# Gate and value of a second pair of blocks as a 2x2 block product with seven products

## The chip, the cores and the metric

The kernel runs on one core of a Trainium2 chip. Its time is the device time of one execution in microseconds (us); the kernel before takes 939.78 us, the median of 3 runs (939.59 to 940.44).

## The reference

Three steps in a row over 4 batches of 576 tokens (2304 rows of 512). *Attention*, 8 heads of 64: a pooled part (queries, keys and values averaged over 4 tokens, full softmax, result repeated 4 times) plus a local part (each token sees 3 tokens to each side). *First layer pair*: `h = x @ w_in` (512 to 2048), `g = max(h,0) + alpha*min(h,0)`, `x = g @ w_out`. *Second layer pair*: rows divided by their root mean square and multiplied by `rms_g`, then `gate = xn @ w_gate`, `val = xn @ w_val` (512 to 1536), result `(gate * sigmoid(gate) * val) @ w_out`. All inputs and the output are float32.

## The kernel before, in words

**Blocks.** The 2304 tokens are 6 blocks of 384; activations lie with features on the 128 partitions and tokens along the free dimension. Each float32 factor is held as two float16 halves, high and low, so a product of one 128-row slice is three matmuls (high x high, high x low, low x high).

**Layer one** (`m1`) takes a block through 16 groups of 128 hidden features: 12 matmuls of 384 columns into a bank `hps` (L1462), the activation, a split into halves `ghl` (L441, L442) and 12 matmuls into four accumulators `acc` (L1479). **Layer two** (`m2`) takes a block through 12 groups f: 12 gate and 12 value matmuls of 384 columns (`gps`, L1602), the gate (L1615 and L1616 with tanh, L1587 with silu), the value (L1619), a split `uhl` (L1622, L1623) and 9 output matmuls of 512 columns into `oacc` (L1631). Its input is first normalised (`rms_tasks`; L1434 to L1437: product, high half, low half).

**Blocks 4 and 5** go through layer two together in `m2_pair`. Gate and value weights over two halves of the 512 features form a 2x2 matrix of blocks, and the halves of the two token blocks another. Their product takes seven block products of 6 matmuls instead of eight for each f (L1825, banks `pa`, `pb`, `pf`), from four sums of weight blocks (`pair_w`, a call for each of four weight tiles; GpSimd makes the full weights L1740, VectorE the differences L1745, ScalarE and VectorE the halves L1668, L1669) and four sums of input blocks (`pair_x`, L1687). After the products come copies out of PSUM on ScalarE (L1830), additions on VectorE (L1833), two silu gates (L1587) and two values (L1841). The output matrix is a seven-product form too (L1803, L1804, L1810, L1813, L1850 to L1858 make its sums; L1908 its products).

**Attention** fills the other engines meanwhile. Blocks 2 to 5 need chunks `local(4)` to `local(11)` of 192 tokens, two for each block: GpSimd multiplies queries with keys (L547) and weights with values (L601), VectorE reduces (L558, L614), TensorE transposes, VectorE adds the pooled part (L650), and ScalarE and VectorE write the block's input `xt` in halves (L441, L442). `down(b)` is the pooled attention of batch b. Chunks, pooled heads and weight loads take turns in three buffers `raw`; `xt` has two.

**Order.** The program order is: layer one of blocks 0 and 1, layer two of 0 and 1, layer one of 2 and 3, layer two of 2, layer one of 4 and 5, layer two of 3, `m2_pair`. The dictionary `feed` gives attention and weight work to a stage, `rms_at` the normalisation. Afterwards `issue_order` puts every engine's instructions in a fixed order: a list scheduler with its own table of costs, whose priorities are path lengths to the end, corrected by the table `LEADS` (range of instruction numbers, ns).

Of the kernel before, what the change touches and what calls it, by code (L numbers as in the profile page):

```python
# [2114 lines left out]
```

## Time and profile before

| | us |
|---|---|
| median of 3 runs | 939.78 |
| the profiled execution | 936.82 |
| its span, first to last instruction | 935.1 |
| TensorE busy | 909.3 |
| VectorE busy | 662.0 |
| ScalarE busy | 520.4 |
| GpSimd busy | 337.7 |

Busy times are sums over the records of an engine. PE is TensorE, PEld its weight loads, DVE VectorE, ACT ScalarE, POOL GpSimd, SP SyncE. A matmul's record includes its way through the array, so records overlap; how far apart they start tells what each costs in a stream. The stages of the second half, from the timeline: layer one of blocks 2 and 3 from 393 us, layer two of 2 from 533, layer one of 4 and 5 from 600 and 665, layer two of 3 from 732, the pair's gates and values from 802, its outputs until the end.

### The profile page before, as it was taken

To read this page: it belongs to the slowest core of one execution; us is meant where nothing else is said; L and a number is where in the kernel's file an instruction comes from. 1 tells how busy PE (TensorE), PEld (TensorE's weight loads), DVE (VectorE), ACT (ScalarE), POOL (GpSimd) and SP (SyncE) were. 2 spreads that over 40 slices of the span, in tenths; PEclk is the share of its full clock that TensorE was granted. 3 is DMA by queue.
4 is the path that set the end of the run, shared out by engine and by line. 5 is a ranking of instruction groups with operands and counts; after the bars stand their busy time and mean duration, and the time that the engine had idled before them with its cause. 6 is when DMAs were issued, how large, how long until landed. Compare 5 with 4: busy or idle time off the path is not lost.

```text
span 935.1 us, 16829 instructions
## 1 busy us (share of the span) xinstructions
PE 909.3 (97%) x6574; PEld 608.4 (65%) x6574; DVE 662.0 (71%) x1257; ACT 520.4 (56%) x1222; POOL 337.7 (36%) x279
## 2 busy tenths in 40 slices
PE   7979999999999999999999999999999999999997
PEld 5768777799755555566666655556666555566686
DVE  4789996797989965788765777387366234478882
ACT  5899999889973365133576232243444332465640
POOL 1101100350436304777224788252132010057750
PEclk9999999999999999999999999999999999999999
DMA  9785445455321232221131211010000000000002
GB/s 243 242 281 171 128 114 178 157 192 195 102 85 60 69 108 70 85 85 60 60 119 36 85 51 34 2 33 1 1 1 1 1 1 1 23 12 1 1 1 68
DMA packets 53713, 73.80 MB, mean 79 GB/s; under 512 B 22190, under 2 KB 35138, under 8 KB 53634
## 3 DMA queue, kind: packets, MB, share of 16 engines
q1 hardware_dynamic: 53634, 72.74, 25.2%
q8 instruction: 51, 0.84, 0.4%
q14 instruction: 28, 0.23, 0.1%
HBM read 68.01 MB, written 4.72 MB: 78 GB/s over the span
## 4 chain that ended last, share of the span: by engine, by line
PE 86%; DMA 4%; ACT 4%; DVE 3%; issue 1%; SPq 0%; POOL 0%; DVEq 0%; ACTq 0%
PE gps L1602 20%; PE acc L1479 18%; PE hps L1462 18%; PE oacc L1631 9%; PE pa L1825 4%; PE px L1908 3%; DMA out_dram<-ob 2%; PE pf L1825 2%; PE py L1908 1%; PE pb L1825 1%; DMA wr<-in_moe_w_in_dram 1%; PE sps L734 1%; PE avps L774 1%; PE lsps L957 1%; DMA wr<-in_moe_w_gate_dram 1%
## 5 line engine op out<-in xcount | busy, mean ns | idle before, releaser
L1462 PE MATMUL hps<-xt,wi 128*128 128x192 f16 (+1 forms) x1536 | 342.0, 289 | 4.1 <-DVE ghl L442 1.2
L1479 PE MATMUL acc<-ghl,wo 128*128 128x384 f16 (+1 forms) x960 | 245.1, 310 | 0.9 <-DVE x L1565 0.4
L1602 PE MATMUL gps<-x,w 128*128 128x384 f16 x1152 | 238.1, 326 | 0.0
L1462 PEld LDWEIGHTS <-wi 128*128 128x128 f16 x1536 | 148.4, 100 | 59.7 <-issue 6.7
L1479 PEld LDWEIGHTS <-wo 128*128 128x128 f16 x1344 | 128.8, 98 | 57.6 <-issue 0.8
L1602 PEld LDWEIGHTS <-w 128*128 128x128 f16 x1152 | 112.5, 99 | 75.5 <-issue 1.4
L1631 PE MATMUL oacc<-w,uhl 128*128 128x512 f16 x432 | 139.7, 379 | 0.0
L547 POOL TENSOR_TENSOR prod<-cq,ckv 128x896 f32<-128x896 f32 x48 | 100.4, 2111 | 74.7 <-PE avps L774 50.8
L1468 DVE SCALAR_TENSOR_TENSOR hps<-g,oma,hps 128x192 f32<-128x192 f32 (+1 forms) x128 | 66.2, 518 | 46.2 <-ACT g L1466 45.5
L601 POOL TENSOR_TENSOR prod<-ls,ckv 128x896 f32<-128x896 f32 x48 | 84.7, 1853 | 28.7 <-DVE lo L614 26.2
L1466 ACT ACTIVATE g<-hps 128x384 f32<-128x384 f32 x96 | 47.2, 491 | 77.4 <-PE hps L1462 76.8
L1631 PEld LDWEIGHTS <-uhl 128*128 128x128 f16 x432 | 42.6, 99 | 41.2 <-ACT uhl L1622 0.2
L1479 PE MATMUL acc<-g,wo 128*128 128x384 f16 (+1 forms) x384 | 68.8, 286 | 0.0
L441 ACT ACTIVATE ghl<-hps,grp 128x384 f16<-128x384 f32 (+1 forms) x73 | 42.1, 577 | 31.9 <-DVE hps L1468 31.4
L442 DVE SCALAR_TENSOR_TENSOR ghl<-hps,grp,ghl 128x384 f16<-128x384 f32 (+1 forms) x73 | 44.3, 607 | 19.0 <-ACT ghl L441 18.9
L558 DVE TENSOR_REDUCE ls<-prod 128x14 f32<-128x896 f32 x48 | 51.7, 1079 | 3.4 <-POOL prod L547 3.3
L614 DVE TENSOR_REDUCE lo<-prod 128x128 f32<-128x896 f32 x48 | 51.8, 1080 | 2.3 <-POOL prod L601 2.0
L1615 ACT ACTIVATE th<-gps,tsc 128x384 f32<-128x384 f32 x36 | 20.7, 579 | 58.7 <-PE gps L1602 58.7
L987 POOL TENSOR_TENSOR dls<-dls,dlsum 96x408 f32<-96x408 f32 x12 | 11.8, 1005 | 110.2 <-ACT g L441 61.4
L1740 POOL TENSOR_TENSOR wt<-w 128x768 f32<-128x768 f16 x16 | 27.4, 1712 | 66.3 <-ACT g L1466 30.4
L1622 ACT ACTIVATE uhl<-gps 128x384 f16<-128x384 f32 x48 | 23.4, 487 | 44.5 <-DVE gps L1619 39.4
L1187 ACT ACTIVATE wr<-wr 128x768 f32<-128x768 f32 (+1 forms) x48 | 42.0, 879 | 4.2 <-DMA wr<-in_moe_w_in_dram 2.1
(332 smaller groups left out, 1682.6 us busy)
## 6 DMA issues: line engine op xcount, KB each, us to landing
wr<-in_moe_w_out_dram SPq DMA_DIRECT2D x18, 512.0 KB
wr<-in_moe_w_in_dram SPq DMA_DIRECT2D x10, 768.0 KB
wr<-in_moe_w_gate_dram SPq DMA_DIRECT2D x8, 768.0 KB
wr<-in_moe_w_val_dram SPq DMA_DIRECT2D x8, 768.0 KB
ckv<-in_k_dram SPq DMA_DIRECT2D x7, 768.0 KB
ckv<-in_v_dram SPq DMA_DIRECT2D x7, 768.0 KB
wr<-in_moe_w_out_dram SPq DMA_DIRECT2D x20, 256.0 KB
sd<-in_q_dram SPq DMA_DIRECT2D x24, 144.0 KB
```

The costliest lines, as they stand in the source:

```text
L442: nc.vector.scalar_tensor_tensor(out=lo, in0=src, scalar=s, in1=hi, op0=ALU.mult, op1=ALU.subtract)
L547: engs[i].tensor_tensor(out=pr, in0=view(st["q"][:, j, t:t + TP], [[D, TP], [0, ND], [1, D]]), in1=view(st["k"][:, j, t:t + TP], [[D, TP], ...
L558: nc.vector.tensor_reduce(out=st["s"][:, j, t:t + TP], in_=st.pop(("p", i)), axis=AX.X, op=ALU.add)
L601: engs[i].tensor_tensor(out=over(pr, i), in0=view(st["s"][:, j, t:t + TP], [[ND, TP], [1, ND], [0, D]]), in1=view(st["v"][:, j, t:t + TP], ...
L614: nc.vector.tensor_reduce(out=st["o"][:, t:t + TP, j], in_=view(pr, [[ND * D, TP], [ND, D], [1, ND]]), axis=AX.X, op=ALU.add)
L1462: nc.tensor.matmul(ps[:, j], wi[:, f + j, a, kk * 128:(kk + 1) * 128], x[:, b_, kk, c0:c0 + n], start=(i == 0), stop=(i == 3 * KK - 1))
L1466: nc.scalar.activation(out=g, in_=ps, func=AF.Relu, scale=-1.0)
L1468: nc.vector.scalar_tensor_tensor(out=ps[:, j], in0=g[:, j], scalar=oma[:, f + j:f + j + 1], in1=ps[:, j], op0=ALU.mult, op1=ALU.add)
L1479: nc.tensor.matmul(acc[e], wo_f(f)[:, a, e * 128:(e + 1) * 128], hl[:, b_], start=(f == f0 and i == 0), stop=(f == f1 and i == 2))
L1602: nc.tensor.matmul(ps, w2_t[i0 + f // 3].rearrange("p a (k c) -> p a k c", k=KK)[:, a, kk, (f % 3) * 128:(f % 3 + 1) * 128], xh[:, b_, kk] ...
L1631: nc.tensor.matmul(acc[tt], t[:, a, tt * 128:(tt + 1) * 128], w[:, b_, f % 3], start=(f in first and i == 0), stop=(f in last and i == 2))
L1825: nc.tensor.matmul(ps, w[:, a, kk, c:c + 128], x[:, b_, kk], start=(start and n == 0), stop=(n == 3 * K2 - 1), skip_group_check=True)
```

## The change

Blocks 2 and 3 become a pair as well (`m2_pair_a`). Their gate and value products take the seven-product form through `pair_f`, which is the loop body of the old `m2_pair` made a function; their outputs are plain products, made after all twelve f from halves kept in `wo`. `m2` is left for blocks 0 and 1. Layer one of blocks 2, 3, 4 and 5 follows in one row, then `m2_pair_a`, then `m2_pair`. The sums of the weight blocks are made once and used by both pairs: the first weight tile's in layer one of block 5, the other three in the first groups of `m2_pair_a`, with scratch in `wo`. `pair_x(p)` makes the normalised inputs and their differences for a pair in pieces of 384 columns; `rms_tasks` of blocks 2 to 5 leaves a copy of the norm factor in SBUF (`r_t`) and no longer multiplies. Block 2's gate is silu in place of tanh. `local(10)` is handed over one stage earlier. Scratch of `m2_pair` moves to other buffers, and `LEADS` is another table (328 entries for 262).

```diff
@@ -22,59 +22,72 @@
 LEADS = (
-    (8269, 8277, -4000), (3290, 3494, -500), (6599, 6626, -500), (7948, 7994, -15500), (5847, 6045, -12500),
...
@@ -1369,6 +1382,8 @@
 
     x1_t = {}
 
+    PAIR = 2
+
             st["r"] = ps
+            if m >= PAIR:
+                st["r"] = r_t[m] = att.tile([128, BW], F32, tag=("xs", "aT")[m % 2], name="rs")
+                nc.scalar.activation(out=r_t[m], in_=ps, func=AF.Copy)
...
-        return [sq(e) for e in range(KK)] + [ssum, bcast] + [xn(e) for e in range(KK)]
+        return [sq(e) for e in range(KK)] + [ssum, bcast] + [xn(e) for e in range(KK) if m < PAIR]
-            tag = ("x1", "xh", "u11")[m % 3]
+            tag = ("x1", "xh", "u11", "x1", "xh", "raw")[m]
-            if m == PAIR - 1:
-                silu(u, gp, f)
-            else:
-                nc.scalar.activation(out=th, in_=gp, func=AF.Tanh, scale=tsc[:, f // 3:f // 3 + 1])
-                nc.vector.scalar_tensor_tensor(out=u, in0=th, scalar=1.0, in1=gp, op0=ALU.add, op1=ALU.mult)
+            nc.scalar.activation(out=th, in_=gp, func=AF.Tanh, scale=tsc[:, f // 3:f // 3 + 1])
+            nc.vector.scalar_tensor_tensor(out=u, in0=th, scalar=1.0, in1=gp, op0=ALU.add, op1=ALU.mult)
...
+    def pair_x(p):
+        ma, mb = PAIR + 2 * p, PAIR + 2 * p + 1
+        last = mb == NBLK - 1
+        st = {}
+
+        def begin():
+            for m in (ma, mb):
+                xh_t[m] = x1_t[m].bitcast(F16).rearrange("p k (a n) -> p a k n", a=2)
+            if p == 0:
+                t12 = xt_p.tile([128, 2, 2, K2, BW], F16, tag="xt", name="xc")
+                t4 = att.tile([128, 2, K2, BW], F16, tag="lo", name="xc")
+                tx[p] = {1: t12[:, 0], 2: t12[:, 1], 3: xh_t[mb][:, :, 0:K2], 4: t4}
+            else:
+                tx[p] = {n: w2_t[3 + n][:, :, 0:PW].rearrange("p a (k n) -> p a k n", k=K2) for n in range(1, 5)}
+
...
+        def y(k, n):
+            def f():
+                if k == n == 0:
+                    begin()
+                if n == 0:
+                    st["y"] = place(k)
+                m, e = (ma, mb)[n // 2], k + K2 * (n % 2)
+                o = st["y"][n]
+                for i in range(NT if m == mb and last else 1):
+                    z = [o, x1_t[m][:, e], r_t[m]]
+                    if m == mb and last:
+                        z = [v[:, i * 128:(i + 1) * 128] for v in z]
+                        z = [z[0].rearrange("p (c t) -> p t c", c=NC)] + [
+                            v.rearrange("p (t c) -> p t c", c=NC) for v in z[1:]]
+                    nc.vector.scalar_tensor_tensor(out=z[0], in0=z[1], scalar=rgx[:, e:e + 1], in1=z[2],
+                                                   op0=ALU.mult, op1=ALU.mult)
+                if n != 2:
+                    halves(xh_t[m][:, 0, e], xh_t[m][:, 1, e], o)
+            return f
+
+        def diff(k, n):
+            def f():
+                b11, b21, b12, b22 = st["y"]
+                o, a, b = ((b11, b12, b11), (b11, b22, b11), (b12, b22, b12), (b21, b21, b11))[n - 1]
+                nc.vector.tensor_tensor(out=o, in0=a, in1=b, op=ALU.subtract)
+                halves(tx[p][n][:, 0, k], tx[p][n][:, 1, k], o)
+            return f
+
+        NT = BW // 128
+        return [t for k in range(K2) for t in [y(k, n) for n in range(4)] + [diff(k, n) for n in range(1, 5)]]
...
+            if i:
+                o = (6 + n) * 2 * BW
+                return wo[:, o:o + PW]
...
+    def pair_f(p, f, scr, done):
...
+        product(A, wv(i, 0), b11, c, True)
+        snap(s1_, A)
+        product(B_, wv(i, K2), b21, c, True)
+        plus(s1_, B_)
+        ga = gate(f, s1_, wk, "mm")
+        product(A, s[1], t[2], c, False)
+        snap(s2_, A)
+        product(F_, s[0], t[1], c, True)
+        product(A, s[2], t[3], c, False)
+        snap(s3_, A)
+        plus(s3_, F_)
+        product(F_, s[3], b22, c, False)
+        plus(s2_, F_)
+        gb = gate(f, s2_, hl_p, "hl")
+        product(A, wv(4 + i, K2), t[4], c, False)
+        done(f, ga, A, gb, s3_)
...
+    def m2_pair_a():
         ma, mb = PAIR, PAIR + 1
         NT = BW // 128
-        scr = [outd_p.tile([128, BW], F32, tag="outd", name="sn") for _ in range(2)]
+        free, scr = ring()
+        ut = xt_p.tile([128, 2, 2, BW], F32, tag="xt", name="uhl")
+        free.extend([outd_p.tile([128, BW], F32, tag="outd", name="sn") for _ in range(2)])
+        spare = [ut[:, 1, 0], ut[:, 1, 1]]
+        free.extend(spare + val_places(0))
+
+        def uhl(f):
+            t = wo[:, f * 2 * BW:(f + 1) * 2 * BW] if f < 10 else ut[:, f - 10].rearrange("p h n -> p (h n)")
+            return t.bitcast(F16).rearrange("p (h a n) -> p h a n", h=2, a=2)
+
+        def done(f, ga, A, gb, s3_):
+            for h, (u, v) in enumerate(((ga, A), (gb, s3_))):
+                value(f, u, u, v)
+                t = uhl(f)[:, h]
+                halves(t[:, 0], t[:, 1], u)
+
+        w_tasks = deque(t for i in (1, 2, 3) for t in pair_w(i))
+        r_tasks = deque(rms_tasks(ma + 2) + rms_tasks(mb + 2))
+        for f in range(NF2):
+            for _ in range(8):
+                if w_tasks:
+                    w_tasks.popleft()()
+            for _ in range(2 if f > 2 else 0):
+                if r_tasks:
+                    r_tasks.popleft()()
+            if f in (3, 6):
+                free.extendleft(val_places(f // 3))
+            if f == 9:
+                kept = [x for x in free if x is not spare[0] and x is not spare[1]]
+                free.clear()
+                free.extend(kept)
+            pair_f(0, f, scr, done)
+        for t in list(r_tasks) + pair_x(1):
+            t()
+        for h, m in enumerate((ma, mb)):
+            for tt in range(NT):
+                n = h * NT + tt
+                tag = ("a0", "at", "w", "a1", "at", "a2")[n]
+                acc = pool_of(tag).tile([128, DM], F32, tag=tag, name="oacc")
+                for f in range(NF2):
+                    w = w2_t[8 + f // 3].rearrange("p a (f e) -> p a f e", f=3)
+                    for i, (a, b_) in enumerate(((0, 0), (0, 1), (1, 0))):
+                        nc.tensor.matmul(acc, uhl(f)[:, h, a, tt * 128:(tt + 1) * 128], w[:, b_, f % 3],
+                                         start=(f == 0 and i == 0), stop=(f == NF2 - 1 and i == 2))
+                tag = ("ob", "da")[n % 2]
+                o = pool_of(tag).tile([128, DM], F32, tag=tag, name="ob")
+                nc.scalar.activation(out=o, in_=acc, func=AF.Copy, scale=col(INV2))
+                rows_out(o, m, tt)
...
+        for f in range(NF2):
+            pair_f(1, f, scr, done)
...
-        ("m1", 3): down(3)+local(9),
-        ("m2", 2): local(10),
+        ("m1", 3): down(3)+local(9)+local(10),
         ("m1", 4): local(11),
-        ("m1", 5): pair_w(0),
-    rms_at = {"o1": 0, ("m2", 0): 1, ("m1", 3): 2, ("m2", 2): 3}
+    rms_at = {"o1": 0, ("m2", 0): 1, ("m1", 3): 2, ("m1", 4): 3}
-        if key == ("m2", 3):
-            urgent.extend(rms_tasks(PAIR) + rms_tasks(PAIR + 1) + pair_x())
-            for i in (1, 2, 3):
-                bg.extend(pair_w(i))
+        if key == ("m1", 5):
+            urgent.extend(pair_x(0) + pair_w(0))
...
-    for kind, m in (("m2", 0), ("m2", 1), ("m1", 2), ("m1", 3), ("m2", 2), ("m1", 4), ("m1", 5), ("m2", 3)):
+    for kind, m in (("m2", 0), ("m2", 1), ("m1", 2), ("m1", 3), ("m1", 4), ("m1", 5)):
...
+    m2_pair_a()
     m2_pair()
```

## Rows read from the trace of the kernel before

**Rows 1.** the page's busy times: engine, us, share of the span, instructions

```profile
PE 909.3 (97%) x6574; PEld 608.4 (65%) x6574; DVE 662.0 (71%) x1257; ACT 520.4 (56%) x1222; POOL 337.7 (36%) x279
```

**Rows 2.** the page's chain that ended last, by engine

```profile
PE 86%; DMA 4%; ACT 4%; DVE 3%; issue 1%; SPq 0%; POOL 0%; DVEq 0%; ACTq 0%
```

**Rows 3.** stretches: start:end, length, each engine's busy us (instructions), clock, DMA share, GB/s

```profile
0.00:238.00 238.00, 220.44 (x2175) 183.58 (x2176) 189.94 (x467) 208.96 (x531) 39.55 (x61) 0.99 0.61 187
...
533.40:600.50 67.10, 67.10 (x393) 38.63 (x391) 43.08 (x71) 20.06 (x44) 50.69 (x37) 1.00 0.15 42
...
665.20:732.10 66.90, 66.90 (x413) 40.30 (x412) 38.04 (x52) 29.55 (x56) 16.61 (x11) 1.00 0.00 1
732.10:802.30 70.20, 70.20 (x414) 40.85 (x412) 30.50 (x57) 26.24 (x49) 4.67 (x5) 1.00 0.00 1
...
846.00:889.60 43.60, 43.60 (x278) 26.95 (x277) 36.26 (x57) 29.44 (x64) 30.77 (x32) 1.00 0.01 2
```

**Rows 4.** timeline of TensorE, 732 to 803 us: start, us, group, count

```profile
732.95 8.13 PE L1602 MATMUL gps<-x,w 128*128 128x384 f16 x49
...
797.97 4.48 PE L1631 MATMUL oacc<-w,uhl 128*128 128x512 f16 x20
```

**Rows 5.** groups by shape, 533 to 601 us: count, busy us, mean ns, idle before

```profile
L1619 DVE SCALAR_TENSOR_TENSOR gps<-th,kap,gps 128x384 f32<-128x384 f32 x11 | 6.8, 618 | 0.4
...
L1616 DVE SCALAR_TENSOR_TENSOR th<-th,gps 128x384 f32<-128x384 f32 x11 | 6.1, 553 | 15.5 <-ACT th L1615 15.5
```

**Rows 6.** groups by shape, 812 to 880 us, the block product

```profile
L1830 ACT ACTIVATE w<-pa 128x384 f32<-128x384 f32 x22 | 10.6, 488 | 8.7 <-PE pa L1825 8.5
...
L1833 DVE TENSOR_TENSOR w<-pf,w 128x384 f32<-128x384 f32 x13 | 7.2, 553 | 1.1 <-PE pf L1825 1.1
...
L1841 DVE SCALAR_TENSOR_TENSOR th<-th,kps,pa 128x384 f32<-128x384 f32 x10 | 6.0, 609 | 1.3 <-PE pa L1825 0.8 <-ACT th L1587 0.3
...
L1804 DVE SCALAR_TENSOR_TENSOR w<-th,w 128x384 f16<-128x384 f32 x3 | 3.2, 1083 | 0.0
...
L1841 DVE SCALAR_TENSOR_TENSOR th<-th,kps,w 128x384 f32<-128x384 f32 x2 | 1.9, 980 | 0.0
```

**Rows 7.** groups of VectorE by shape, 734 to 803 us

```profile
L1687 DVE TENSOR_TENSOR wo<-wo 128x768 f32<-128x768 f32 x4 | 3.8, 951 | 0.0
L1669 DVE TENSOR_TENSOR x<-wo,x 128x384 f16<-128x384 f32 x6 | 3.3, 554 | 0.2
...
L1669 DVE TENSOR_TENSOR wsx<-wt,wsx 128x768 f16<-128x768 f32 x2 | 1.8, 952 | 0.0
```

**Rows 8.** groups by shape, 577 to 650 us, VectorE and GpSimd

```profile
L1745 DVE TENSOR_TENSOR wt<-wt 128x768 f32<-128x768 f32 x8 | 8.8, 1099 | 0.0
...
L1669 DVE TENSOR_TENSOR wsr<-wt,wsr 128x768 f16<-128x768 f32 x4 | 6.1, 1528 | 0.0
...
L1740 POOL TENSOR_TENSOR wt<-w 128x768 f32<-128x768 f16 x8 | 13.7, 1711 | 13.4 <-DVE wt L1745 7.6 <-DVE wsr L1669 4.7 <-DVE lo L614 1.0
```

**Rows 9.** timelines of GpSimd and of VectorE, 634 to 640 us

```profile
636.14 1.64 POOL L1740 TENSOR_TENSOR wt<-w 128x768 f32<-128x768 f16 x1 [2.35 <-DVE wt L1745]
...
636.45 2.15 DVE L1745 TENSOR_TENSOR wt<-wt 128x768 f32<-128x768 f32 x1
```

**Rows 10.** timeline of TensorE, 526 to 536 us: first product of block 2's second layer

```profile
533.41 0.33 PE L1602 MATMUL gps<-x,w 128*128 128x384 f16 x1
```

**Rows 11.** timeline of VectorE, 533 to 543 us: last write of block 4's input

```profile
541.97 0.62 DVE L442 SCALAR_TENSOR_TENSOR xt<-xps,sc,xt 128x384 f16<-128x384 f32 x1
```

**Rows 12.** timeline of GpSimd, 418 to 605 us; in brackets the idle time before

```profile
438.15 10.56 POOL L601 TENSOR_TENSOR prod<-ls,ckv 128x896 f32<-128x896 f32 x6
...
500.27 2.08 POOL L547 TENSOR_TENSOR prod<-cq,ckv 128x896 f32<-128x896 f32 x1 [6.70 <-PE avps L774]
...
522.78 10.28 POOL L601 TENSOR_TENSOR prod<-ls,ckv 128x896 f32<-128x896 f32 x6
```

**Rows 13.** the page's costly groups: attention's products on GpSimd

```profile
L547 POOL TENSOR_TENSOR prod<-cq,ckv 128x896 f32<-128x896 f32 x48 | 100.4, 2111 | 74.7 <-PE avps L774 50.8
```

More of the change, by code (lines that the diff above doesn't have):

```diff
@@ L1419, in f @@
                     xh_t[m] = x1_t[m].bitcast(F16).rearrange("p k (a n) -> p a k n", a=2)
-                if m >= PAIR:
-                    y = pair_y(m, e)
-                    for i in range(NT if m > PAIR else 1):
-                        z = [y, x1_t[m][:, e], st["r"]]
-                        if m > PAIR:
-                            z = [v[:, i * 128:(i + 1) * 128] for v in z]
-                            z = [z[0].rearrange("p (c t) -> p t c", c=NC)] + [
-                                v.rearrange("p (t c) -> p t c", c=NC) for v in z[1:]]
-                        nc.vector.scalar_tensor_tensor(out=z[0], in0=z[1], scalar=rgx[:, e:e + 1], in1=z[2],
-                                                       op0=ALU.mult, op1=ALU.mult)
-                    if m == PAIR or e >= KK // 2:
-                        halves(xh_t[m][:, 0, e], xh_t[m][:, 1, e], y)
-                    return
                 x = x1_p.tile([128, BW], F32, tag=("ra", "rb")[e % 2], name="ra")
@@ L1661, in m2 @@
             rows_out(o, m, tt)
-    PAIR = NBLK - 2
     K2 = KK // 2
@@ L1669, in halves, with place @@
         nc.vector.tensor_tensor(out=lo, in0=x, in1=hi, op=ALU.subtract)
-    def pair_y(m, e):
-        o = 6 * 2 * BW + ((m - PAIR) * KK + e) * BW
-        return wo[:, o:o + BW]
     tx = {}
-    def pair_x():
-        t12, t34 = (xt_p.tile([128, 2, 2, K2, BW], F16, tag="xt", name="xc") for _ in range(2))
-        tx.update({1: t12[:, 0], 2: t12[:, 1], 3: t34[:, 0], 4: t34[:, 1]})
-        def y(m, h):
-            return wo[:, 6 * 2 * BW + ((m - PAIR) * KK + h * K2) * BW:][:, 0:K2 * BW]
-        b11, b21, b12, b22 = y(PAIR, 0), y(PAIR, 1), y(PAIR + 1, 0), y(PAIR + 1, 1)
-        def sub(o, a, b):
-            nc.vector.tensor_tensor(out=o, in0=a, in1=b, op=ALU.subtract)
-        def put(n, x):
-            halves(tx[n][:, 0], tx[n][:, 1], x.rearrange("p (k n) -> p k n", k=K2))
-        def f1():
-            sub(b11, b12, b11)
-            put(1, b11)
-        def f2():
-            sub(b11, b22, b11)
-            put(2, b11)
-        def f3():
-            sub(b12, b22, b12)
-            put(3, b12)
-        def f4():
-            sub(b21, b21, b11)
-            put(4, b21)
-        return [f1, f2, f3, f4]
+    def pair_x(p):
[11 more added lines that the diff above has]
+                tx[p] = {n: w2_t[3 + n][:, :, 0:PW].rearrange("p a (k n) -> p a k n", k=K2) for n in range(1, 5)}
+        def place(k):
+            if p == 0:
+                t = [prod_p.tile([128, 2, BW], F32, tag="prod", name="yt") for _ in range(2)]
+                return [t[n // 2][:, n % 2] for n in range(4)]
+            tag = ("u11", "x1")[k]
+            t = pool_of(tag).tile([128, 4, BW], F32, tag=tag, name="yt")
+            return [t[:, n] for n in range(4)]
+        def y(k, n):
[26 more added lines that the diff above has]
+        return [t for k in range(K2) for t in [y(k, n) for n in range(4)] + [diff(k, n) for n in range(1, 5)]]
@@ L1721, in pair_dst @@
             return wi.rearrange("p f a c -> p (f a c)")[:, o:o + 2 * PW].rearrange("p (a w) -> p a w", a=2)
[L1722 to L1724 removed]
+        sw["x", u] = prod_p.tile([128, PW], F32, tag="prod", name="wsp")
+        return sw["x", u].bitcast(F16).rearrange("p (a w) -> p a w", a=2)
     def pair_w(i):
@@ L1751, in pair_w, with wv, product @@
                 comb(2, 0, 3, 0, ALU.subtract), comb(4, 1, 1, 0, ALU.subtract)]
-    def m2_pair():
+    def wv(i, k0):
+        return w2_t[i].rearrange("p a (k c) -> p a k c", k=KK)[:, :, k0:k0 + K2]
+    def product(ps, w, x, c, start):
+        n = 0
+        for kk in range(K2):
+            for a, b_ in ((0, 0), (0, 1), (1, 0)):
+                nc.tensor.matmul(ps, w[:, a, kk, c:c + 128], x[:, b_, kk], start=(start and n == 0),
+                                 stop=(n == 3 * K2 - 1), skip_group_check=True)
+                n += 1
@@ new lines, in snap, with plus, gate, value @@
+    def snap(o, ps):
+        nc.scalar.activation(out=o, in_=ps, func=AF.Copy)
+    def plus(o, ps):
+        nc.vector.tensor_tensor(out=o, in0=ps, in1=o, op=ALU.add)
+    def gate(f, g, pool, tag):
+        th = pool.tile([128, BW], F32, tag=tag, name="th")
+        silu(th, g, f)
+        return th
+    def value(f, o, u, v):
+        nc.vector.scalar_tensor_tensor(out=o, in0=u, scalar=kps[:, f // 3:f // 3 + 1], in1=v, op0=ALU.mult,
+                                       op1=ALU.mult)
+    def pair_f(p, f, scr, done):
+        xa, xb = xh_t[PAIR + 2 * p], xh_t[PAIR + 2 * p + 1]
+        b11, b21, b22 = xa[:, :, 0:K2], xa[:, :, K2:KK], xb[:, :, K2:KK]
+        t = tx[p]
+        i, c = f // 3, f % 3 * 128
+        s = [sw[i, n].rearrange("p a (k c) -> p a k c", k=K2) for n in range(1, 5)]
+        s1_, s2_, s3_ = scr(), scr(), scr()
+        ta, tb, tf = f"a{f % 3}", "at", ("w", "w", "a3")[f % 3]
+        A = pool_of(ta).tile([128, BW], F32, tag=ta, name="pa")
+        B_ = pool_of(tb).tile([128, BW], F32, tag=tb, name="pb")
+        F_ = pool_of(tf).tile([128, BW], F32, tag=tf, name="pf")
+        product(A, wv(i, 0), b11, c, True)
[14 more added lines that the diff above has]
+        done(f, ga, A, gb, s3_)
@@ L1754, in m2_pair, with ring, take, val_places @@
+    def ring():
+        places = deque()
+        def take():
+            places.rotate(-1)
+            return places[-1]
+        return places, take
+    def val_places(i):
+        return [w2_t[4 + i][:, a, 0:PW].bitcast(F32) for a in range(2)]
+    def m2_pair_a():
         ma, mb = PAIR, PAIR + 1
         NT = BW // 128
-        scr = [outd_p.tile([128, BW], F32, tag="outd", name="sn") for _ in range(2)]
+        free, scr = ring()
[43 more added lines that the diff above has]
+                rows_out(o, m, tt)
@@ L1757, in m2_pair @@
+    def m2_pair():
+        ma, mb = PAIR + 2, PAIR + 3
+        NT = BW // 128
+        free, scr = ring()
         lo = att.tile([128, 2, BW], F32, tag="lo", name="sn")
-        scr += [lo[:, 0], lo[:, 1]]
-        for i in range(4):
-            scr += [w2_t[4 + i][:, a, 0:PW].bitcast(F32) for a in range(2)]
+        sct, zt = [xt_p.tile([128, 4, BW], F32, tag="xt", name="sn") for _ in range(2)]
+        free.extend([outd_p.tile([128, BW], F32, tag="outd", name="sn") for _ in range(2)])
+        free.extend([lo[:, 0], lo[:, 1]] + [sct[:, i] for i in range(4)])
@@ L1778, in places @@
         def places():
-            r = raw_p.tile([128, 4 * BW], F32, tag="raw", name="us").bitcast(F16)
+            r = x1_p.tile([128, 4 * BW], F32, tag="x1", name="us").bitcast(F16)
             S3.extend(part(r, n) for n in range(3))
@@ L1816, in wsums @@
             scaled(wof(g)[:, :, ED:DM], b1, 1.0)
-        def wv(i, k0):
-            return w2_t[i].rearrange("p a (k c) -> p a k c", k=KK)[:, :, k0:k0 + K2]
-        def product(ps, w, x, c, start):
-            n = 0
-            for kk in range(K2):
-                for a, b_ in ((0, 0), (0, 1), (1, 0)):
-                    nc.tensor.matmul(ps, w[:, a, kk, c:c + 128], x[:, b_, kk], start=(start and n == 0),
-                                     stop=(n == 3 * K2 - 1), skip_group_check=True)
-                    n += 1
-        def snap(o, ps):
-            nc.scalar.activation(out=o, in_=ps, func=AF.Copy)
-        def plus(o, ps):
-            nc.vector.tensor_tensor(out=o, in0=ps, in1=o, op=ALU.add)
-        def gate(f, g, pool, tag):
-            th = pool.tile([128, BW], F32, tag=tag, name="th")
-            silu(th, g, f)
-            return th
-        def value(f, o, u, v):
-            nc.vector.scalar_tensor_tensor(out=o, in0=u, scalar=kps[:, f // 3:f // 3 + 1], in1=v, op0=ALU.mult,
-                                           op1=ALU.mult)
         def usums(f, ga, gb):
@@ L1856, in usums @@
             G.tensor_tensor(out=y, in0=gb, in1=y, op=ALU.subtract)
-            z = prod_p.tile([128, BW], F32, tag="prod", name="s4")
+            z = zt[:, g % 4]
             G.tensor_tensor(out=z, in0=ga, in1=y, op=ALU.subtract)
@@ L1861, in usums, with done @@
             scaled(two(S4[g]), z, 0.25)
[L1863 to L1887 removed]
+        def done(f, ga, A, gb, s3_):
             value(f, ga, ga, A)
```

31 lines of the change are left out of this document (2 added, 29 removed), and 118 rows, old and new, of the table LEADS.

## The prediction

> **What bounds the kernel now.** I read the page's busy times first: TensorE is busy 909.3 of 935.1 us, and no other engine reaches 75% [rows 1]. A busy TensorE can still be waiting, so I read the chain of waits next: 86% of the way to the last instruction is TensorE work [rows 2]. Then I cut the span into the kernel's stages: from 238 us to the end of the gate and value products TensorE is full in every stage (67.1 of 67.1, 66.9 of 66.9, 70.2 of 70.2, 43.6 of 43.6 us), while VectorE stands between 43% and 83% [rows 3]. Only before 238 us is there idle time, 238.0 - 220.4 = 17.6 us, in work that the change doesn't edit.
>
> Last, the timeline tells what one matmul costs when they stream. A record lasts 0.33 us, but 49 in a row take 8.13 us, so one begins every (8.13 - 0.33) / 48 = 0.1625 us with 384 columns; 20 in a row with 512 columns give (4.48 - 0.38) / 19 = 0.2158 us [rows 4]. The granted clock is full there. So in this half of the kernel time is the number of columns fed to TensorE, and each matmul that goes is worth its spacing, if nothing else becomes late.
>
> **The change, part by part.** *Products.* Blocks 2 and 3 each had 12 x 2 x 12 gate and value matmuls, together 576. The block product needs 7 products of 6 matmuls for each of 12 column groups, 504. 72 x 0.1625 = 11.7 us leave TensorE's stream. The output products stay: 216 matmuls of 512 columns. Transposes, sums of squares and layer one keep their counts.
>
> The Trainium skill, "TensorE: Matmul & The Clock Gate", section "Back-to-back issue gap", gives for streams with weight loads 81 ns at 128 columns and 131 ns at 512; an estimate between the two for 384 columns is 114 ns, and the saving by it would be 8.2 us. The spacings above (0.1625 and 0.2158 us, with a weight load for each) contradict it, so the trace decides.
>
> *Work behind the products.* For each column group, blocks 2 and 3 together had five VectorE operations and four on ScalarE: 0.55 us for the tanh product (block 2 only) and, in each block, 0.62 us for the value and 0.55 us for the low half, 2.9 us on VectorE [rows 5, 7]. Now it is three additions at 0.553, two values at 0.609 and two low halves at 0.554: 1.66 + 1.22 + 1.11 = 3.99 us [rows 6, 7]; the sum over 12 groups grows by 13 us. ScalarE gets three more copies at 0.488 us [rows 6], 18 us in all. The stage's matmuls take 42 x 0.1625 = 6.83 us a group, so both are covered if nothing else wants VectorE then.
>
> *But the weight sums move into that stage.* Those of the second to fourth weight tiles were made beside layer one of block 5, where VectorE is busy 38.0 of 66.9 us [rows 3]. Now their scratch lies in the layer-one output weights and their results in the layer-one input weights, so they can begin only as layer one of block 5 ends, and each must be ready three groups after the one before. One tile costs four GpSimd additions of 1.71 us [rows 8], and four VectorE differences at 0.951 and four low halves at 0.952, 7.6 us [rows 7]. In three groups, 20.5 us of TensorE, VectorE has 3 x 3.99 + 7.6 = 19.6 us to do. That cover is nearly gone before any collision. And there are collisions: a VectorE difference that starts while GpSimd adds takes 2.15 us and not 0.95: it began 0.31 us into GpSimd's 1.64 us and ended 0.82 us after it [rows 9]. Bounds for the stage: nothing lost if the order puts GpSimd's 6.8 us under the additions and values out of PSUM; at the other end every operation with two SBUF operands at the dearest mean price that rows show: 1.66 + 0.609 + 0.98 + 2 x 1.083 = 5.42 us a group and 4 x 1.10 + 4 x 1.53 = 10.5 us a tile [rows 6, 8], so 26.8 us in 20.5, 6.3 us late three times, 18.9 us. I take 2 us: the stage most like it (846 to 889.6 us) has GpSimd busy 30.8 and VectorE 36.3 of 43.6 us, and TensorE lost nothing there [rows 3]; that is nearer to the lower end, but 19.6 of 20.5 is more than 83%. Behind a product that waits for its sum stand all later products, and the outputs behind them; three of a group's seven need no sum, 18 matmuls or 2.9 us that can go ahead.
>
> The Trainium skill, "GPSIMD Engine Reference", section "Key points", says that GpSimd shares its SBUF interfaces with VectorE and meets instructions with two SBUF inputs. The 2.15 us agree; the rule speaks against putting the sums here.
>
> *Input sums.* For blocks 2 and 3, eight multiplications, eight copies and eight GpSimd subtractions become eight multiplications, six and eight low halves and eight differences on VectorE, 8 x 0.609 + 22 x 0.554 = 17.1 us [rows 6, 7]. Their place is layer one of block 5, where the weight sums (7.6 us a tile, three tiles) have left, so they are covered. For blocks 4 and 5 the same work runs while TensorE makes 216 x 0.2158 = 46.6 us of outputs, with VectorE otherwise free: nothing.
>
> *Layer one in a row.* Taking the second layer of block 2 out from between removes 70 us in which attention for block 4 could finish. TensorE's work up to layer one of block 3 ends at 533.4 us [rows 10]; the last write of block 4's input ended at 541.97 + 0.62 = 542.6 us [rows 11]. With the same order TensorE would wait 9.2 us; the upper bound. Below it is zero: the products of the chunk before ended at 448.7 us, those of this chunk waited until 500.3 us (GpSimd idle 6.70 us, freed by the pooled attention of batch 3) [rows 12], and part of what was in the way, the normalisation of block 2's input, is gone from there. Nothing asked for the chunk before 600 us; now it leads. I take 0. Block 5 needs two more chunks in one layer-one time, 65 us: 24 products at 2.11 us at most are 51 us of GpSimd [rows 13]; it fits, and the loads of the first of them are issued one stage earlier, behind those of batch 3's pooled attention as before.
>
> *The rest.* The norm factors are copied out of PSUM (four copies on ScalarE), the output rows of blocks 2 and 3 are issued in one stage, where SyncE has nothing else left to load (DMA share 0.00 from 665 us on [rows 3]), scratch lies elsewhere: all off TensorE, nothing. The corrections to the issue order are all replaced; in the 17.6 us idle before 238 us that can gain or cost a little, I take 0 and keep 1.5 us either way.
>
> **Sum.** The profiled execution took 936.82 us (span 935.1 and 1.7 around it), 2.96 below the median of the runs, 939.78. 936.82 - 11.7 + 2.0 = 927.1; on the scale of the medians 930.1 us. Its own range is 926.5 (no wait, order 1.5 better) to 933.
>
> **Rivals.**
> 1. *VectorE becomes the bound in the gate stage of blocks 2 and 3* (the slower side). Place: the first nine column groups. At 26.8 us for 20.5 it costs 18.9 us: 939.78 - 11.7 + 18.9 = 947.0. It decides against the change from 20.5 + 11.7 / 3 = 24.4 us in three groups. For it: 19.6 us before collisions. Against: the fuller GpSimd at 846 us without loss. 10%.
> 2. *The same at half price*: 23.2 us in 20.5, 2.7 us three times, 8 us: 936.1. 12%.
> 3. *Attention is late at block 4*, 9.2 us: 937.3. For it: chunk end against need. Against: idle GpSimd ahead of it. 10%.
> 4. *The page's spacing*: 939.78 - 8.2 = 931.6, with no wait added. The rows speak against it. 4%.
> 5. *The saving doesn't arrive*: the other order loses in the first 238 us or at the joints what the products save: 939.8. 5%.
>
> **How the numbers follow.** The forecast has the remaining 59%. 0.2%, 1.9 us, is about what a measurement of this kernel can tell from no change. Forecast, rivals 2 and 4 and most of 3 are faster: 83%; rival 5 and the rest of 3, 7%; rival 1, 10%. The range goes from 926.5 to 938.5 us; rival 1, rival 5 and some 3% below are left out.
>
> **What would show it.** Right: TensorE's busy time falls by about 11.7 us to 898; 1008 block-product matmuls stand for 504, 576 plain ones for 1152; the stage from the first to the last gate product of blocks 2 and 3 lasts about 82 to 84 us with TensorE full; VectorE's total grows by some 25 us (13 and 12) and the time still falls. Rival 1 or 2: in that stage TensorE waits for VectorE or its sums, at the fourth, seventh or tenth column group, and differences and low halves last over 1.5 us. Rival 3: a gap in layer one's first product of block 4, ended by the input's split. Rival 4: the spacing within a run of block products. Wrong altogether: TensorE's busy time unchanged, or idle time before 238 us grown by several us.

## The result and the profile after

The changed kernel takes 925.05 us (median of four runs, 924.39 to 925.36); the kernel before took 939.84 beside it (939.59 to 940.44). The ratio is 0.9841, with a 95% interval from 0.9824 to 0.9858: 14.8 us faster, where 9.7 were forecast. Its profiled execution took 925.22 us, with a span of 923.3 and 1.9 around it. From one profiled execution to the other it is 936.82 - 925.22 = 11.6 us, so the difference between 11.6 and 14.8 lies between the profiled execution and the median of the kernel before, not between the two traces.

The page's busy times and its chain by engine, after:

```profile
PE 896.1 (97%) x6502; PEld 600.5 (65%) x6502; DVE 682.2 (74%) x1311; ACT 538.6 (58%) x1272; POOL 345.5 (37%) x271
...
PE 88%; ACT 5%; DVE 2%; DMA 2%; SPq 1%; POOL 1%; issue 1%; DVEq 0%; ACTq 0%
```

Against [rows 1, 2]: TensorE has 72 matmuls and 13.2 us fewer, VectorE 20.2 us more, and the path is still TensorE's. By the names in the trace 1008 block products and 576 plain gate and value matmuls are there, as forecast.

The stretches after, in the columns of [rows 3]: the start, layer one of block 4, layer one of block 5 with the first products of blocks 2 and 3 between it, the first third of the dense part of their gate stage, all of that dense part, and the end of the gate and value products of blocks 4 and 5.

```profile
0.00:238.00 238.00, 219.45 (x2184) 183.88 (x2185) 190.50 (x469) 207.80 (x530) 43.45 (x61) 0.99 0.60 184
530.20:595.10 64.90, 64.90 (x411) 40.57 (x408) 51.17 (x85) 26.40 (x57) 48.33 (x34) 1.00 0.12 31
602.00:669.00 67.00, 65.89 (x406) 39.55 (x405) 36.56 (x56) 29.89 (x62) 13.45 (x9) 1.00 0.00 1
669.00:690.00 21.00, 21.00 (x133) 12.73 (x131) 18.79 (x27) 14.75 (x28) 10.38 (x5) 1.00 0.01 2
669.00:732.80 63.80, 63.80 (x406) 39.92 (x404) 54.42 (x84) 41.42 (x81) 22.18 (x13) 1.00 0.01 1
846.00:889.00 43.00, 43.00 (x306) 29.75 (x305) 38.36 (x55) 28.23 (x63) 31.62 (x28) 1.00 0.01 2
```

The two rows at 669 us are the ones to look at: VectorE is busy 54.42 of 63.80 us, 85%, and 18.79 of 21.00, 89%, in the first third; GpSimd works beside it, and TensorE has lost nothing. The only idle place of the whole stage is 1.11 us at its beginning, where the first products wait until ScalarE has copied layer one's output out of PSUM:

```profile
668.36 0.81 PE L1781 MATMUL pa<-x,w 128*128 128x384 f16 x4 [1.11 <-ACT x L1503]
```

The matmuls still stream at their old spacing (TensorE's timeline: start, us, group, count), (1.30 - 0.33) / 6 = 0.162 us as in [rows 4]:

```profile
800.85 1.30 PE L1781 MATMUL pb<-x,w 128*128 128x384 f16 x7
```

The joint at block 4, which [rows 10 to 12] put in doubt; timelines of TensorE (its first product of block 4's layer one), VectorE (last write of block 4's input) and GpSimd:

```profile
530.21 0.33 PE L1468 MATMUL hps<-xt,wi 128*128 128x384 f16 x1
...
529.33 0.61 DVE L455 SCALAR_TENSOR_TENSOR xt<-xps,sc,xt 128x384 f16<-128x384 f32 x1
...
490.50 2.08 POOL L560 TENSOR_TENSOR prod<-cq,ckv 128x896 f32<-128x896 f32 x1 [21.75 <-DMA ckv<-in_k_dram]
...
512.19 10.48 POOL L614 TENSOR_TENSOR prod<-ls,ckv 128x896 f32<-128x896 f32 x6
```

The chunk began its products 9.8 us earlier than before (490.5 against 500.3), released by a load and no longer by the pooled attention, and the input was written at 529.9 us, not 542.6. TensorE went on without a break.

Groups by shape in the dense part, 669 to 732.8 us:

```profile
L1761 POOL TENSOR_TENSOR wo<-w 128x768 f32<-128x768 f16 x8 | 16.2, 2045 | 19.1 <-DVE wo L1766 7.6 <-ACT wi L1670 7.1 <-DVE wi L1671 4.4
L1671 DVE TENSOR_TENSOR wi<-wo,wi 128x768 f16<-128x768 f32 x10 | 11.9, 1200 | 0.0
L1671 DVE TENSOR_TENSOR wo<-th,wo 128x384 f16<-128x384 f32 x17 | 9.1, 552 | 0.7 <-ACT wo L1670 0.6
...
L1766 DVE TENSOR_TENSOR wo<-wo 128x768 f32<-128x768 f32 x9 | 9.1, 1008 | 0.0
...
L1797 DVE SCALAR_TENSOR_TENSOR th<-th,kps,pa 128x384 f32<-128x384 f32 x9 | 5.5, 610 | 3.1 <-PE pa L1781 3.1
L1789 DVE TENSOR_TENSOR w<-pf,w 128x384 f32<-128x384 f32 x9 | 5.0, 554 | 1.6 <-PE pf L1781 0.9 <-ACT w L1786 0.6
...
L1797 DVE SCALAR_TENSOR_TENSOR th<-th,kps,uhl 128x384 f32<-128x384 f32 x4 | 3.8, 954 | 0.0
```

The prices are those of [rows 6, 7], and the meetings with GpSimd that were feared do happen. They cost 10 x (1.200 - 0.952) + 9 x (1.008 - 0.951) + 4 x (0.954 - 0.609) = 4.4 us over these groups, and VectorE's work still fits. The counterpart to [rows 9], on GpSimd and VectorE:

```profile
688.40 3.83 POOL L1761 TENSOR_TENSOR wo<-w 128x768 f32<-128x768 f16 x2 [7.60 <-DVE wo L1766]
...
690.96 2.09 DVE L1671 TENSOR_TENSOR wi<-wo,wi 128x768 f16<-128x768 f32 x1
```

The low half takes 2.09 us for 0.95 and ends 0.82 us after GpSimd's pair, the same picture as before.

### The profile page after: what moved, and what is told of

It reads as the page before. It is cut to its first block, busy times and chain, and to the rows that moved or that the text cites. A ratio compares the mean times of both kernels' runs of the same rounds, so it can differ in the third digit from the quotient of the medians.

```text
span 923.3 us, 16796 instructions
## 1 busy us (share of the span) xinstructions
PE 896.1 (97%) x6502; PEld 600.5 (65%) x6502; DVE 682.2 (74%) x1311; ACT 538.6 (58%) x1272; POOL 345.5 (37%) x271
## 4 chain that ended last, share of the span: by engine, by line
PE 88%; ACT 5%; DVE 2%; DMA 2%; SPq 1%; POOL 1%; issue 1%; DVEq 0%; ACTq 0%
PE acc L1485 20%; PE hps L1468 18%; PE gps L1608 10%; PE pa L1781 9%; PE oacc L1884 5%; PE oacc L1634 5%; PE pf L1781 5%; PE px L1999 3%; PE pb L1781 2%; PE py L1999 1%; PE avps L787 1%; ACT wi L454 1%; ACT wr L1200 1%; PE lsps L970 1%; DMA wr<-in_moe_w_in_dram 1%; PE sps L747 1%
## 5 line engine op out<-in xcount | busy, mean ns | idle before, releaser
L1468 PE MATMUL hps<-xt,wi 128*128 128x192 f16 (+1 forms) x1536 | 322.7, 288 | 4.2 <-ACT wi L454 2.4
L1485 PE MATMUL acc<-ghl,wo 128*128 128x384 f16 (+1 forms) x960 | 227.6, 310 | 0.0
L1468 PEld LDWEIGHTS <-wi 128*128 128x128 f16 x1536 | 147.6, 100 | 56.2 <-issue 3.1
L1608 PE MATMUL gps<-x,w 128*128 128x384 f16 x576 | 126.5, 326 | 0.9 <-DVE uhl L1626 0.9
L614 POOL TENSOR_TENSOR prod<-ls,ckv 128x896 f32<-128x896 f32 x48 | 88.3, 1918 | 5.8 <-DVE lo L627 5.0
L1608 PEld LDWEIGHTS <-w 128*128 128x128 f16 x576 | 56.5, 99 | 38.2 <-issue 1.9
L1634 PE MATMUL oacc<-w,uhl 128*128 128x512 f16 x216 | 73.5, 379 | 0.0
L1781 PEld LDWEIGHTS <-w 128*128 128x128 f16 x432 | 42.4, 99 | 29.6 <-issue 2.0
L1000 POOL TENSOR_TENSOR dls<-dls,dlsum 96x408 f32<-96x408 f32 x12 | 11.7, 998 | 118.3 <-DVE dlsum L997 106.6
L1948 POOL TENSOR_TENSOR wr<-w 128x512 f32<-128x512 f16 x12 | 15.8, 1321 | 96.1 <-ACT th L1593 89.3
L1781 PEld LDWEIGHTS <-wi 128*128 128x128 f16 x360 | 35.2, 98 | 22.8 <-issue 0.4
L1884 PE MATMUL oacc<-w,wo 128*128 128x512 f16 x180 | 48.5, 379 | 0.0
L1781 PE MATMUL pa<-x,w 128*128 128x384 f16 x144 | 46.4, 326 | 1.1 <-ACT x L1503 1.1
```

What stands on the lines that cost most here:

```text
L614: engs[i].tensor_tensor(out=over(pr, i), in0=view(st["s"][:, j, t:t + TP], [[ND, TP], [1, ND], [0, D]]), in1=view(st["v"][:, j, t:t + TP], ...
L1468: nc.tensor.matmul(ps[:, j], wi[:, f + j, a, kk * 128:(kk + 1) * 128], x[:, b_, kk, c0:c0 + n], start=(i == 0), stop=(i == 3 * KK - 1))
L1485: nc.tensor.matmul(acc[e], wo_f(f)[:, a, e * 128:(e + 1) * 128], hl[:, b_], start=(f == f0 and i == 0), stop=(f == f1 and i == 2))
L1608: nc.tensor.matmul(ps, w2_t[i0 + f // 3].rearrange("p a (k c) -> p a k c", k=KK)[:, a, kk, (f % 3) * 128:(f % 3 + 1) * 128], xh[:, b_, kk] ...
L1634: nc.tensor.matmul(acc[tt], t[:, a, tt * 128:(tt + 1) * 128], w[:, b_, f % 3], start=(f in first and i == 0), stop=(f in last and i == 2))
L1781: nc.tensor.matmul(ps, w[:, a, kk, c:c + 128], x[:, b_, kk], start=(start and n == 0), stop=(n == 3 * K2 - 1), skip_group_check=True)
```

## The experiments

**Both kernels once more.** No edit; on one chip, beside the next two.

> The kernel before, unchanged, to see how its executions spread. Its profiled execution took 936.82 us with a span of 935.1 us; its other runs took 939.6 to 940.4 us. Theory (that execution was an unusually short one): most runs take 939.5 to 940.5 us with spans near 938 us, so that a profile taken in such a run shows 3 us more inside the span. Rival (the profile is typical and the runs carry 3 us outside the span): spans stay near 935 us while the times are near 940 us.

> The kernel after, unchanged. Theory: times 924.4 to 925.5 us with spans 922.5 to 923.6 us in every run, as in the four runs before, so that its profiled execution is a typical one. Rival: it spreads as the kernel before does, and further runs lie 3 us higher, near 928 us.

The kernel before took 938.6 us (12 runs, 936.59 to 941.84) and 938.27 (23 runs, 936.39 to 943.55) as reference; the kernel after 926.09 (four runs, 925.20 to 928.32), ratio 0.9862, interval 0.9838 to 0.9887. The gain is there again, at 12.2 us. A run's span lies some 1.7 us below its time throughout (936.8 for 938.54, 941.8 for 943.55), so what spreads lies inside the span. Both theories missed on the numbers all the same: most runs of the kernel before stayed under 939.5, and three of the four of the kernel after went over 925.5. The profiled 936.82 that the sum started from lies near the lower edge of what the kernel before does; the profiled 925.22 of the kernel after lies among its first four runs and at the lower edge of these four.

**Seventy-two products more.** The order of all other instructions is kept; the lines that see to it are left out of this diff and of the next two.

```diff
         product(B_, wv(i, K2), b21, c, True)
+        if p == 0:                     # blocks 2 and 3 alone
+            product(B_, wv(i, K2), b21, c, True)
```

> The kernel after with the order of all its instructions kept; in the gate stage of blocks 2 and 3 the second product of each group is made twice (72 more matmuls of 384 columns, eight products for seven). Theory (TensorE's columns set the time of this stage): 72 x 0.1625 = 11.7 us more, 936.7 us. Rival (the stage waits for VectorE or for the weight sums, and TensorE has spare time): less than 6 us more, under 931 us.

935.76 us (10 runs, 934.41 to 936.66), 9.7 above the kernel after beside it; 72 x 0.1625 = 11.7. The busy times:

```profile
PE 907.2 (97%) x6574; PEld 607.2 (65%) x6574; DVE 683.8 (73%) x1311; ACT 538.5 (58%) x1272; POOL 345.3 (37%) x271
```

TensorE grew by 907.2 - 896.1 = 11.1 us and the span by 934.0 - 923.3 = 10.7; the idle 1.11 us at the stage's beginning is gone, so 11.7 less that is 10.6. By the spans each product taken out is worth its spacing; the medians, 2.0 us short of 11.7, say so less sharply. The kernel has the product columns of the kernel before and is still 2.5 us faster than it (ratio 0.9968, interval 0.9954 to 0.9981): that much of the gain is not the products.

**One product of seven a third as wide.** It leaves out that product's term for 256 of its 384 columns, in blocks 2 and 3.

```diff
-        product(A, s[2], t[3], c, False)
+        if p == 0:
+            product(A[:, 0:128], s[2], t[3][:, :, :, 0:128], c, False)
+        else:
+            product(A, s[2], t[3], c, False)
```

> The kernel after with the order of all its instructions kept; in the gate stage of blocks 2 and 3 the fifth product of each group (third weight sum times third input sum) covers 128 of its 384 columns, so that gate and value of the other columns lack that term. 72 matmuls are 256 columns shorter, 72 x 256 / 2400 = 7.7 us. Theory (columns set the time): 917.4 us. Rival (VectorE, busy 18.8 of 21.0 us in three groups there, or the weight sums take over): less than 4 us saved, 921 us or more.

918.36 us (917.84 to 918.98), 7.7 below the kernel after beside it: 72 matmuls, 0.107 us each, for two thirds of 0.1625 = 0.108. Time goes with the columns. With the spacings that the Trainium skill ("TensorE: Matmul & The Clock Gate", section "Back-to-back issue gap") gives for streams with weight loads, an estimate of 114 ns less 81, it would have been 2.4 us; the run decides against them here. And VectorE, whose work did not shrink, let TensorE go through the stage in 7.7 us less, so it had at least that much to spare.

**Two doses of VectorE work.** Each of the 24 low halves of the stage is made once more (0.555 us each), then twice more, with the order of all else kept.

```diff
                 halves(t[:, 0], t[:, 1], u)
+                for _ in range(1):     # the second dose: range(2)
+                    nc.vector.tensor_tensor(out=t[:, 1], in0=u, in1=t[:, 0], op=ALU.subtract)
```

> The kernel after, its order kept, with each of the 24 low halves that the first pair's gate stage makes written one more time by VectorE (0.555 us each, 13.3 us in all, 1.1 us per group of seven products; every term is still there). In the dense part of that stage VectorE was busy 18.8 of 21.0 us per three groups, so 2.2 us were free and 3.3 are asked. Theory 'VectorE has a reserve of a tenth there and does not set the pace': little or nothing, 925 to 929 (at most 1.1 us for each of the three such stretches). Rival 'VectorE already sets the pace through its waits on the products' (the first rival of the prediction in a weaker form): the whole 13.3 us, 938.

> The same with two more of each (26.6 us in all, 6.7 us asked per three groups where 2.2 were free). Theory 'reserve of a tenth': now VectorE sets the pace in the three dense stretches, (6.7 - 2.2) x 3 = 13.5 us less what the working buffers hold over to the stretch behind, 932 to 939. Rival 'VectorE already sets the pace': 26.6 us, 952. Rival 'the buffers carry it all into the lighter stretches' (103.8 of 151 us busy in the whole of the stage, 130 with these): nothing, 925 to 927.

930.27 us (ratio to the kernel before 0.9903, interval 0.9884 to 0.9921) and 940.78 (1.0016, 1.0004 to 1.0028). Against the 0.9862 of the kernel after, which ran on another chip, that is some 3.8 us for a dose of 13.3, and 14.4 for 26.6; the intervals allow almost 3 us either way. Both lie 1 to 2 us above the range of the theory "reserve" and 8 to 11 below "VectorE already sets the pace"; that the buffers carry all of it falls too. The dense stretch, first dose and second, in the columns of [rows 3]:

```profile
669.00:732.80 63.80, 60.08 (x374) 36.85 (x373) 60.11 (x93) 38.41 (x75) 21.80 (x13) 1.00 0.00 1
```

```profile
669.00:732.80 63.80, 56.50 (x350) 34.54 (x350) 60.77 (x93) 38.00 (x75) 22.15 (x13) 1.00 0.00 1
...
733.00:736.00 3.00, 0.46 (x2) 0.25 (x2) 2.90 (x7) 0.00 (x0) 0.00 (x0) 0.76 0.00 0
736.00:738.00 2.00, 2.00 (x8) 0.88 (x6) 1.97 (x4) 0.36 (x1) 0.00 (x0) 0.50 0.00 0
738.00:742.00 4.00, 4.00 (x16) 1.95 (x15) 1.49 (x4) 1.16 (x3) 0.00 (x0) 0.58 0.00 0
```

VectorE stops at about 60 of 63.8 us, 94 to 95%, and TensorE loses 3.7 and 7.3 us there where it lost none at 85%. So rival 1's mechanism exists, and it begins before VectorE is full: 17 of the 24 low halves lie in this stretch, so the first dose asks 17 x 0.555 = 9.4 us there, as much as was free; VectorE took up 60.1 - 54.4 = 5.7, and the other 3.7 are what TensorE lost. The second dose is dearer also by the clock. TensorE was busy 0.46 of the 3 us up to 736, at the end of a wait of 4.01 us for a VectorE sum:

```profile
735.54 0.48 PE L1798 MATMUL pf<-x,wi 128*128 128x384 f16 x1 [4.01 <-DVE uhl L1806]
```

The granted clock is 0.76 in these 3 us, so it fell to half (1.2 of 2.4 GHz) 3.0 x 0.24 / 0.5 = 1.4 us before their end, within the wait. It stayed there for the next 2.0 us and was 0.58 on the mean of the four behind, so TensorE worked 0.46 + 2.0 + 4.0 x 0.42 / 0.5 = 5.8 us at the lower level, of which half, 2.9 us, is lost. In the whole stage the traces of the two doses have 3.9 and 11.3 us of TensorE's waits that the kernel after has not; 2.9 and 7.8 of them end in a VectorE instruction, the others in a ScalarE copy out of PSUM. With the clock that makes 3.9 and 14.2 us, close to what the ratios give.

**The order of the first 232 us exchanged.** Each kernel takes the other's order there (3,048 instructions in the kernel before, 3,067 in the kernel after), then its own.

```diff
-    for q in best[1].values():
+    for e, q in best[1].items():
+        head = HEAD.get(e, ())  # the other kernel's order up to 232 us
+        q = list(head) + [k for k in q if k not in set(head)]
```

> The kernel before, with one thing exchanged: on each engine the instructions of the first 232 us (embedding, the first attention, block 0 and the start of block 1; 3,048 of them without the loads of weights) stand in the order that the kernel after has there, behind them its own order. Theory 'the order of the head makes the offset' (before's runs lie 1 to 3 us above its profiled execution, after's do not): 936 to 937.5, 1 to 2.5 us below the kernel before beside it, and a narrow spread, as the kernel after has. Rival 'it is spread that goes with the chip and the moment': no difference from the kernel before (within 0.7 us) and its spread. A third, 'it arises later than 232 us': no difference either; the exchanged head of the other kernel tells the last two apart no further.

> The converse: the kernel after with before's order in the first 232 us. Theory 'the order of the head makes the offset': 927 to 928.5, 1 to 2.5 us above the unchanged kernel after, with a wider spread. Rival 'it goes with the chip and the moment' or 'it arises later': 925 to 926.5, as the kernel after.

The kernel before became slower: 942.91 us against 938.91 beside it (ratio 1.0037, interval 1.0021 to 1.0053), the opposite of what my theory asked. The kernel after took 927.58 (926.68 to 927.66; ratio 0.987, interval 0.9851 to 0.9889, which overlaps that of the kernel after unchanged): a time inside my theory's range, a spread that isn't wider. The timeline of TensorE in the kernel before with the exchanged head, with its idle times in brackets:

```profile
243.61 1.31 PE L1624 MATMUL acc<-ghl,wo 128*128 128x192 f16 x12 [1.49 <-ACT ghl L586]
249.28 2.77 PE L1747 MATMUL gps<-x,w 128*128 128x384 f16 x9 [2.31 <-ACT x L1642]
```

At the seam ScalarE still has conversions of weights ahead of the activations, and TensorE waits in these two places. Behind the second it also ran at half clock (granted 0.50 between 251 and 253 us; its nine matmuls there took 2.77 us). They are the seam's, not the head's, so this half doesn't answer the question. For the converse, stretches of the kernel before, of the kernel after with before's head, and of the kernel after:

```profile
100.00:240.00 140.00, 137.58 (x1457) 116.74 (x1455) 114.67 (x266) 125.97 (x297) 29.70 (x23) 1.00 0.50 158
```

```profile
100.00:240.00 140.00, 137.66 (x1461) 117.00 (x1460) 114.73 (x268) 125.81 (x301) 27.83 (x22) 1.00 0.49 154
```

```profile
100.00:240.00 140.00, 138.90 (x1478) 118.32 (x1477) 115.64 (x267) 123.67 (x288) 32.98 (x22) 1.00 0.50 153
```

With before's order TensorE does 1.2 to 1.3 us less there in these three profiles. But the five other profiles of the kernel before have 137.77 to 138.34 us in this stretch, and the kernel before with after's head has 137.72: the kernel after is ahead by 0.6 to 1.3 us, and its head alone doesn't carry that over. A part of it also makes up for a later start: by 80 us the kernel after had issued 493 matmuls, the profile of before 504. So the head's part of the offset is not shown.

**The kernel before, profiled four times more.**

> The unchanged kernel before, profiled once more, to catch an execution in the upper part of its spread (936.4 to 943.6). Theory 'order of VectorE and GpSimd where both work on an attention' (in one execution VectorE's reduction at 444.8 us met a GpSimd product, took 1.99 us, and TensorE lost 1.2 us behind it; in the profile read for the prediction they did not meet): an execution 1.5 us or more above 936.8 shows its excess as one to four idle places of TensorE of 0.5 to 2 us between 160 and 530 us, behind a VectorE instruction lengthened by GpSimd. Rival 'the clock': it shows more or longer stretches at half clock, each of some 3.4 us costing about 1.7. Rival 'loading': idle places behind DMA transfers in the first 120 us.

> As the look before it: whichever of the three (places in 160 to 530 us behind lengthened VectorE work; half clock; loading in the first 120 us) carries the excess of an execution over 936.8.

> As the look before it: whichever of the three carries the excess of an execution over 936.8.

> As the look before it: whichever of the three carries the excess of an execution over 936.8.

938.56, 937.91, 936.98 and 938.75 us. With 936.82 and 938.54 these are six profiled executions of the kernel before, and the one that I predicted from is the fastest. Three places carry the excess. In the second look, and in the profile of the repeated run, a VectorE addition of the pooled attention met a GpSimd product of the local one. GpSimd, VectorE and TensorE in the second look:

```profile
444.27 1.84 POOL L601 TENSOR_TENSOR prod<-ls,ckv 128x896 f32<-128x896 f32 x1
...
444.27 1.97 DVE L711 TENSOR_TENSOR qkp<-sd 72x256 f32<-72x256 f32 x1
...
450.54 1.14 PE L1462 MATMUL hps<-xt,wi 128*128 128x384 f16 x6 [1.02 <-DVE ghl L442]
```

The same three in the profile of before:

```profile
444.90 3.81 POOL L601 TENSOR_TENSOR prod<-ls,ckv 128x896 f32<-128x896 f32 x2
...
444.92 0.41 DVE L711 TENSOR_TENSOR qkp<-sd 72x256 f32<-72x256 f32 x1
...
450.12 0.65 PE L1462 MATMUL hps<-xt,wi 128*128 128x384 f16 x3 [0.35 <-DVE ghl L442]
```

The two start within 0.02 us of each other each time. Once VectorE gets through in 0.41 us, once it needs 1.97 and ends 0.13 us after GpSimd; behind it TensorE is idle 1.02 us and not 0.35. In the first and fourth look it is the start; the first 80 us of the profile of before and of the fourth look:

```profile
0.00:80.00 80.00, 65.65 (x504) 51.92 (x505) 57.73 (x156) 65.65 (x183) 7.31 (x31) 0.96 0.85 256
```

```profile
0.00:80.00 80.00, 63.03 (x484) 49.27 (x485) 55.86 (x148) 63.80 (x176) 7.31 (x31) 0.98 0.84 249
```

Twenty matmuls fewer by 80 us, at no lower clock. That is the third theory's place, and a transfer stands out there, in the profile of before and in the fourth look:

```profile
13.56 0.28 PE L2016 MATMUL vecps<-ident,rows 16*128 16x16 f32 x1 [0.92 <-DMA rows<-in_moe_alpha_dram]
```

```profile
14.91 0.28 PE L2016 MATMUL vecps<-ident,rows 16*128 16x16 f32 x1 [2.12 <-DMA rows<-in_moe_alpha_dram]
```

This wait is 2.06 to 2.15 us in the first and fourth look and in the repeated run, 1.53 in the third look, none in the second. No run tells whether it alone makes the twenty matmuls. Half clock explains none of them: in the second look its share was larger,

```profile
0.00:80.00 80.00, 66.12 (x506) 52.39 (x507) 57.62 (x157) 66.12 (x184) 7.31 (x31) 0.89 0.85 254
```

and by 80 us it had issued two matmuls more than the profile of before. The third place, which no theory named, is the end. The last three stores of output rows as SyncE issues them, in the profile of before and in the second look:

```profile
927.22 2.94 SPq L1949 DMA_DIRECT2D out_dram<-ob  x3
```

```profile
927.61 3.56 SPq L1949 DMA_DIRECT2D out_dram<-ob  x3
```

The last of the three takes 0.54 us to issue in the one and 1.16 in the other. From VectorE's last write to the end of the span it is 5.5 us in the profile of before and in the third and fourth look, and 6.2 to 6.3 in the first, the second and the repeated run; in all seven profiles of the kernel after and its variants it is 5.1 to 5.2. No execution of the kernel before above 939 us was caught in a profile; what the slower ones (up to 943.55) lose stays open.

## Why the prediction missed

The direction and the mechanism of the saving were right; the time fell 1.5 us below the range, 5.0 below the forecast. Two terms make the 5.0, the 2.0 us of stall and the 2.96 us of offset.

- *The 2 us taken for a crowded VectorE in the gate stage of blocks 2 and 3* were wrong: 0. I held 19.6 us of VectorE work against 20.5 of TensorE. Measured it is 54.4 in 63.8 for three such stretches, 18.8 in 21.0 in the fullest, and the two doses show that TensorE begins to lose between 89% and 94% in this stage. The stretch was also longer than I reckoned: the input's squares and transposes of blocks 4 and 5 pass through TensorE there, so three groups took about 63.8 / 3 = 21.3 us. And the dearest prices, which I took for every operation at the upper end, hit only some.
- *The 2.96 us from the profiled execution to the median* were carried over whole to the kernel after, which has -0.2 in the first comparison and 0.9 against the repeated runs. One execution stood for the kernel before, and it was its fastest of six. By the mean of the other five, (938.54 + 938.56 + 937.91 + 936.98 + 938.75) / 5 = 938.15, 1.3 of the 2.96 are the choice of execution; the rest differs by chip and moment (medians of 939.84, 938.27 and 938.91) and by a gain of the new kernel that isn't the products, 2.5 us in the run with seventy-two more. Of that gain the traces show 0.3 to 1.1 us behind VectorE's last write and 0.6 to 1.3 between 100 and 240 us. What share each has was not settled.
- *72 x 0.1625 = 11.7* held: 10.7 and 1.1 of idle time with the products put back, 7.7 of 7.7 when one is narrowed. That the two first profiles lie 11.6 apart is partly luck: from the mean of before's six, 937.93, to that of after's two, 925.49, it is 12.4. Rival 4, the spacing of the Trainium skill, falls with it.
- *Attention at block 4, costed at 0* held: its input was there 530.21 - 529.94 = 0.3 us before TensorE took it, because the chunk led by 9.8 us. An estimate that no run tests: without that lead it would have been there at 529.9 + 9.8 = 539.7 us, 9.5 too late, near rival 3's 9.2.
- *Input sums, norm factors, output rows: nothing* held; no TensorE wait stands at any of them but the 1.11 us at the beginning of the stage.
- *The corrections to the issue order: 0, 1.5 either way*: between 100 and 240 us the traces lie 0.6 to 1.3 us on the favourable side; that the order is the cause wasn't shown.
- *What would show it*: TensorE's busy time 896.1 for "to 898", VectorE's growth 20.2 for "some 25". The "82 to 84 us" of the stage can't be read, because its first groups run between the matmuls of block 5's layer one, from 602 us on.

The range failed with the second term: it gave the stall and the order their lower ends (2.0 and 1.5 us) and the offset none, though the runs shown then were three.

## What to carry over

Where TensorE is full on both sides of a change, as here, the column count gives what the products save. In this stage VectorE cost nothing at 85 to 89% busy and 3.7 us at 94%; a stall of 2 us was spent too early. Predict from the spread of the runs and not from the distance of one profiled execution to the median: that distance belongs to the execution. And when instructions are transplanted between two orders, look at the seam before reading the time.
